# Normed rows turned over by transposing DMAs in place of identity products and VectorE copies (tiles 4 to 15)

## The chip, the cores and the metric

The kernel runs on one core of a Trainium2 chip. The metric is the device time of one execution in microseconds (us); of several runs the median is taken. The engines are called as in the profile: PE is TensorE, PEld its weight loads, DVE is VectorE, ACT is ScalarE, POOL is GpSimd, SP is SyncE, which here only issues DMAs.

## The reference

The input x has 2048 rows of 512. It is normed once, and two branches read the normed rows xn; their sum is added to x.

```python
def _layernorm(x, axis=-1, eps=1e-5):
    m = jnp.mean(x, axis=axis, keepdims=True)
    v = jnp.var(x, axis=axis, keepdims=True)
    return (x - m) / jnp.sqrt(v + eps)

# _A_ref: H = 32 heads of Dh = 16
qkv = (x @ wqkv).reshape(B, S, 3, H, Dh).transpose(2, 0, 3, 1, 4)
q, k, v = qkv[0], qkv[1], qkv[2]
p = softmax(einsum("bhqd,bhkd->bhqk", q, k) * Dh ** -0.5)
o = einsum("bhqk,bhkd->bhqd", p, v)
o.transpose(0, 2, 1, 3).reshape(B, S, D) @ wo

# _B_ref: a two-layer MLP over the rows' axis
h = _layernorm(x)
u = gelu(einsum("bsd,sf->bdf", h, w1) + b1)
(einsum("bdf,fs->bds", u, w2) + b2).transpose(0, 2, 1)

xn = _layernorm(x)
x + _A_ref(xn, wqkv, wo) + _B_ref(xn, w1, b1, w2, b2)
```

All tensors are bf16. The products with wqkv need xn with its 512 features on the partitions, that is, xn turned over; the MLP needs it as it is.

## The kernel before

The 2048 rows are 16 tiles of 128. Each tile t has a slice `xn_sb[:, t, :]` (128 rows by 512 features) and a slice of `xnT4` (128 features by 4 blocks of features by 128 rows), its turned-over copy. For tiles 0 to 3 a prologue turns every tile over by itself. For tiles 4 to 15 this is done in pairs, while attention is already running on the tiles that are there.

For such a pair (a, a + 1) the steps are: statistics (`ln_stats`, DVE) and the reciprocal deviation (`ln_rstd`, ACT, two small instructions, lines 611 and 614); the norm (`ln_norm`, DVE, line 630); `tr_steps`, which turns both tiles over; `kt_steps`, the K products of the pair (PE, four groups of four matmuls) and their copy (DVE); and `v_steps`, the V products of each tile (PE) with a copy and a scaling (DVE). `tr_steps` has three steps: `transpose_pe` for the one tile and for the other (PE, four products with the identity `ident` each, line 687, into one bank of PSUM), and `transpose_copy` (DVE, line 700), which copies the two turned tiles from PSUM to `xnT4`. `kt_mm` and `v_mm` (both through `mm_full`, line 667) and `qt_mm` read `xnT4`.

Attention goes by blocks of 512 queries and four heads: `score_mm` (PE, line 770) writes scores into banks of PSUM, `exp_tile` (ACT, line 783) takes one to three banks at a time, `pv_mm` (PE, line 795) multiplies by V. Some exponentials are instead made on DVE and POOL (`first_planes` and `make_plane`, lines 847 and 857).

The order of all this from the first K products on is written out by hand in the string `ORDER`, which `replay` reads: a letter C with a chain's number takes the next step of that chain (the chains are the lists of steps above, in the order of `chains`), S issues scores, E an exponential, P four products with V. The order of the string is thus the program order of every engine: PE, DVE, ACT, POOL and SP each run their own instructions strictly in that order. `Sched.add` records every operation with the keys that it reads and writes; `Sched.plan` turns each dependence on another engine, or on a DMA, into a semaphore wait of the later instruction. A DMA is an operation of the engine that issues it: SP waits for what the DMA needs, and all that SP has to issue later stands behind it. `q_steps` has such DMAs: it spreads the Q rows of two blocks of heads over `QT` (`QT<-qraw`), and the first of them stands between tiles 13 and 14 in the program.

When a chain's first step is taken, the string also names its PSUM bank. For the six `tr` chains this bank is written by the identity products and freed by the copy.

Later in the program `ln2_norm` scales `xn_sb` in place for the MLP (line 644), and the memory of `x_sb`, `xn_sb` and three quarters of `xnT` is used again for planes of the exponentials.

Of the kernel before, what the change touches and what calls it, by code (L numbers as in the profile page):

```python
# [430 lines left out]
def bass_parallel_sum__softmax_full_mha__mixer_token_mlp__prompt_kernel(  # L431
# [18 lines left out]
    with ExitStack() as es:  # L450
        block = es.enter_context(nc.Block())

        def sb(name, shape, dt):
            return es.enter_context(nc.sbuf_tensor(name, shape, dt))
# [3 lines left out]
        x_sb = x_flat[:, :].rearrange("p (t d) -> p t d", d=D)  # L458
        xn_sb = xn_flat[:, :].rearrange("p (t d) -> p t d", d=D)
# [3 lines left out]
        xnT4 = xnT_flat[:, :].rearrange("p (b ct n) -> p b ct n", b=NQB, ct=NCT)  # L463
# [29 lines left out]
        mv = sb("mv", [128, NT, 4], F32)  # L493
# [7 lines left out]
        sc = Sched(nc, es)  # L501
# [20 lines left out]
        for j in range(32):  # L522
# [6 lines left out]
               writes=[("jcol",)])  # L529
        for q in range(4):  # L530
            sl = slice(32 * q, 32 * q + 32)
            sc.add("dve", lambda e, sl=sl: e.tensor_tensor(ident[sl, sl], jrow[sl, 0, :], jrow[sl, 1, :], ALU.is_equal),
                   reads=[("jcol",), ("ident0",)] + [("jrow", j) for j in range(32)], writes=[("ident", q)])
# [93 lines left out]
                          reads=[("x", t), ("nmean", t)], writes=[("mv", t), ("qraw", 1)])  # L627

        def ln_norm(t):
            return sc.add("dve", lambda e: e.tensor_scalar(xn_sb[:, t, :], x_sb[:, t, :], mv[:, t, 0:1], mv[:, t, 2:3],  # L630
                                                           ALU.add if t == T_ACT else ALU.subtract, ALU.mult),
                          reads=[("x", t), ("mv", t), ("rs", t)], writes=[("xn", t)])

        def ln2_scales():
            rk = [("rs", t) for t in range(NT)]
            sc.add("dve", lambda e: e.tensor_tensor(mv[:, :, 3], mv[:, :, 2], mv[:, :, 2], ALU.mult),
                   reads=rk, writes=[("s2",)])
            sc.add("act", lambda e: e.activation(mv[:, :, 3], mv[:, :, 3], ACTF.Ln, bias=epsb[:, 1:2], scale=-EPS),
                   reads=[("s2",), ("epsb", 1)], writes=[("s2",)])
            return sc.add("act", lambda e: e.activation(mv[:, :, 3], mv[:, :, 3], ACTF.Exp, scale=-0.5),  # L640
                          reads=[("s2",)], writes=[("s2",)])
# [42 lines left out]
        def transpose_pe(t, bk, off):  # L684
            op = None
            for ct in range(NCT):
                op = sc.add("pe", lambda e, ct=ct: e.transpose(
                    ps_bf[:, bk * 1024 + off + ct * 128: bk * 1024 + off + (ct + 1) * 128],
                    xn_sb[:, t, ct * 128:(ct + 1) * 128], ident[:]),
                    reads=[("xn", t)] + [("ident", q) for q in range(4)], writes=[("bank", bk)])  # L690
            return op
# [5 lines left out]
        def copy(eng, dst, src, reads, writes):  # L697
            if eng == "act":
                return sc.add("act", lambda e: e.activation(dst, src, ACTF.Identity), reads, writes)
            return sc.add("dve", lambda e: e.tensor_copy(dst, src), reads, writes)  # L700

        def transpose_copy(t0_, n_, bk, eng):
            c0 = 128 * (t0_ % 4)
            dst = xnT4[:, t0_ // 4, :, c0:c0 + 128 * n_].rearrange("p ct (t j) -> p t ct j", t=n_)
            src = ps_bf[:, bk * 1024: bk * 1024 + 512 * n_].rearrange("p (t ct j) -> p t ct j", t=n_, ct=NCT)
            return copy(eng, dst, src, [("bank", bk)], [("xnT", t) for t in range(t0_, t0_ + n_)])
# [184 lines left out]
        ln_var_act(T_ACT)  # L891
        ln_stats(1)
        ln_norm(0)
        transpose_pe(0, TBK[0], 0)
        zeros(N_ZERO1)
        ln_rstd(1, 2)
        ln_stats(3)
        ln_norm(1)
        transpose_pe(1, TBK[1], 0)
        const_v(0, 1)  # L900
        ln_rstd(2, 3)
        transpose_copy(0, 1, TBK[0], "dve")
        ln_norm(2)
        pro_q(0)
        transpose_pe(2, TBK[2], 0)
# [25 lines left out]
            return [lambda bk, t=t: ln_stats(t) for t in (a, a + 1) if t > 4] + [fin]  # L931

        def tr_steps(t0_):
            z = [lambda bk, i=i: transpose_pe(t0_ + i, bk, 512 * i) for i in range(2)]
            return z + [lambda bk: transpose_copy(t0_, 2, bk, "dve")]

        def kt_steps(T, t0_, n_):
            return [lambda bk, ct=ct: kt_mm(T, t0_, n_, ct, bk) for ct in range(NCT)] + [
# [105 lines left out]
        def yo_steps(st, idx):  # L1044
            qb, sti = divmod(st, 4)
            ob = idx % 2
            lastqb = qb == NQB - 1

            def yt(ft, bk):
                if ft == 0:  # L1050
                    dma("sp", xres[:, ob, :], x2[128 * st:128 * (st + 1), :], reads=[], writes=[("xres", ob)])
                yt_mm(bk, st, ft, ft == 0, lastqb and ft == NFT - 1)
                if ft == NFT - 1 and not lastqb:
                    w2_load()
            z = [lambda bk, ft=ft: yt(ft, bk) for ft in range(NFT)]
            if not lastqb:
                z += [lambda bk, T=T: op_mm(qb, sti, T, bk, False, T == 3) for T in range(4)]

                def fin(bk):
                    sc.add("dve", lambda e: e.tensor_tensor(osb[:, ob, :], bank(bk), xres[:, ob, :], ALU.add),  # L1060
                        [("bank", bk), ("xres", ob)], [("osb", ob)])
                    dma("sp", out2[128 * st:128 * (st + 1), :], osb[:, ob, :], reads=[("osb", ob)], writes=[("out", st)],
                        out_dma=True)
            else:
                def fin(bk):
                    sc.add("dve", lambda e: e.tensor_tensor(part[:, sti, :], bank(bk), xres[:, ob, :], ALU.add),
                        [("bank", bk), ("xres", ob)], [("part", sti), ("w1blk", 0), ("w1blk", 1)])
            return z + [fin]
# [69 lines left out]
        for a in range(4, NT, 2):  # L1138
            chains += [tr_steps(a), kt_steps(0, a, 2), v_steps(a, 2, 0, 1)]
# [18 lines left out]
        for i, st in enumerate(yt_order):  # L1158
            z = yo_steps(st, i)
# [228 lines left out]
```

## Time and profile before

| | us |
|---|---|
| median of 3 runs | 627.82 |
| lowest and highest of them | 627.67, 628.01 |
| the profiled execution, its whole time | 627.77 |
| its span (first to last instruction) | 626.0 |

| engine | busy us | share of the span | instructions |
|---|---|---|---|
| PE | 616.7 | 99% | 8777 |
| ACT | 614.2 | 98% | 698 |
| DVE | 584.1 | 93% | 909 |
| POOL | 431.5 | 69% | 624 |

Of the span, the first 9.5 us are the prologue up to the first scores. The tiles 4 to 15 are normed from 13.2 us (tile 4) to 34.2 us (tile 15) and turned over between 14.7 and 36.2 us. The granted TensorE clock is full throughout (0.999 on the mean).

In the rows shown below, a row of the time line has the start and the length in us, the engine, the line of the kernel, the operation, the tile it writes and the tiles it reads, their shapes, and how many instructions in a row were merged into it; in brackets stands the idle time of the engine before it and what ended that. Consecutive rows of one engine can overlap a little, since the next instruction is started before the last has ended. "SPq" is the time for which SP was issuing a DMA, not the time of the transfer. A row of the DMA issues has the number of issues, the size of one and, last, the median time from issue to landing.

### The profile page before, as it was taken

The numbers are of one execution on the slowest core, as the hardware profiler recorded it, in microseconds if no ns is written. First come the engines' busy times: TensorE is split into PE (matmuls) and PEld (weight loads), VectorE is DVE, ScalarE is ACT, GpSimd is POOL, SyncE is SP. The second block draws the span as 40 slices with busy tenths as digits, with TensorE's granted clock in tenths as the row PEclk, the third lists the DMA queues.
The fourth block names the chain that finished last, engine by engine and source line by source line (L and its number), as shares of the span: only waits on it lengthen the run. The fifth ranks groups of instructions, "written<-read, shape, count | busy, mean of one in ns | idle before, by whom it ended". The sixth has DMA issues, their size and how long they took to land.

```text
span 626.0 us, 20540 instructions
## 1 busy us (share of the span) xinstructions
PE 616.7 (99%) x8777; PEld 195.3 (31%) x8777; DVE 584.1 (93%) x909; ACT 614.2 (98%) x698; POOL 431.5 (69%) x624
## 2 busy tenths in 40 slices
PE   8999999999999999999999999999999999999997
PEld 3544333232222222222323332222222222322222
DVE  7999999989999999999999988998989999999996
ACT  8999999999999999999999999999999999999996
POOL 2105766766767767769789777777857788888784
PEclk9999999999999999999999999999999999999999
DMA  8001210112202121030120031213131021222001
GB/s 237 4 12 40 50 54 6 39 39 55 54 11 63 37 66 40 21 78 12 28 52 24 18 87 38 60 39 76 42 91 42 19 59 46 50 52 67 20 27 45
DMA packets 69514, 29.74 MB, mean 48 GB/s; under 512 B 56182, under 2 KB 66422, under 8 KB 69422
## 3 DMA queue, kind: packets, MB, share of 16 engines
q1 hardware_dynamic: 68990, 28.03, 18.3%
q8 instruction: 69, 1.13, 0.8%
q10 hardware_dynamic: 432, 0.39, 0.2%
q14 instruction: 23, 0.19, 0.1%
HBM read 21.88 MB, written 2.59 MB: 39 GB/s over the span
## 4 chain that ended last, share of the span: by engine, by line
PE 82%; ACT 11%; DVE 6%; issue 0%; POOL 0%; DVEq 0%; POOLq 0%
PE ps L795 33%; PE ps L770 28%; PE ps L667 20%; ACT pT L783 8%; ACT wqkv_sb L783 3%; DVE planes L847 1%; DVE x_sb L847 1%; DVE xn_sb L847 1%; DVE stats L604 1%; DVE xn_sb L630 0%; DVE xnT L700 0%; DVE xnT L847 0%; DVE zer L1086 0%; ACT mv L611 0%; ACT mv L614 0%
## 5 line engine op out<-in xcount | busy, mean ns | idle before, releaser
L783 ACT ACTIVATE pT<-ps 128x1024 bf16<-128x1024 f32 (+2 forms) x488 | 459.7, 1034 | 2.2 <-PE ps L770 1.5
L770 PE MATMUL ps<-QT,KT 32*128 32x512 bf16 x2048 | 253.3, 384 | 1.5 <-ACT pT L783 0.4
L847 DVE TENSOR_SCALAR planes<-ps 128x512 int16<-128x512 f32 (+1 forms) x268 | 200.2, 776 | 14.7 <-PE ps L660 6.9
L783 ACT ACTIVATE wqkv_sb<-ps 128x1024 bf16<-128x1024 f32 (+2 forms) x172 | 174.8, 1039 | 0.1
L795 PE MATMUL ps<-pT,V 128*32 128x512 bf16 x950 | 157.7, 386 | 0.6 <-DVE V L700 0.6
L847 DVE TENSOR_SCALAR x_sb<-ps 128x512 int16<-128x512 f32 (+1 forms) x190 | 139.7, 765 | 8.0 <-PE ps L770 3.2
L770 PEld LDWEIGHTS ps<-QT,KT 32*128 32x128 bf16 x2048 | 65.9, 91 | 238.2 <-ACT pT L783 145.8
L795 PE MATMUL ps<-planes,V 128*32 128x512 bf16 x574 | 116.1, 384 | 0.0
L795 PE MATMUL ps<-x_sb,V 128*32 128x512 bf16 x477 | 98.1, 383 | 0.0
L857 POOL INT64_ADD planes<-planes x79 | 60.5, 771 | 43.3 <-DVE planes L847 36.4
L795 PE MATMUL ps<-wqkv_sb,V 128*32 128x512 bf16 x335 | 83.3, 386 | 0.0
L795 PE MATMUL ps<-planes,V17b 128*32 128x512 bf16 x314 | 77.4, 384 | 0.1
L857 POOL INT64_ADD planes<-x_sb x80 | 59.2, 745 | 23.6 <-DVE x_sb L847 22.0
L847 DVE TENSOR_SCALAR xnT<-ps 128x512 int16<-128x512 f32 (+1 forms) x89 | 69.4, 808 | 1.3 <-PE ps L660 0.6
L857 POOL INT64_ADD x_sb<-planes x64 | 53.0, 832 | 20.3 <-DVE planes L847 17.6
L847 DVE TENSOR_SCALAR xn_sb<-ps 128x512 int16<-128x512 f32 (+1 forms) x73 | 58.3, 816 | 4.5 <-PE ps L770 2.9
L795 PE MATMUL ps<-x_sb,V17b 128*32 128x512 bf16 x219 | 56.8, 384 | 0.0
L667 PE MATMUL ps<-gT,w2blk 128*32 128x512 bf16 (+1 forms) x688 | 53.0, 383 | 0.0
L795 PEld LDWEIGHTS ps<-pT,V 128*32 128x32 bf16 x950 | 39.3, 94 | 38.2 <-issue 35.1
L667 PE MATMUL ps<-xn_sb,w1blk 128*32 128x512 bf16 x624 | 50.4, 383 | 0.0
L795 PE MATMUL ps<-xnT,V 128*32 128x512 bf16 x204 | 49.0, 383 | 0.0
L795 PE MATMUL ps<-xn_sb,V 128*32 128x512 bf16 x203 | 43.8, 383 | 0.0
(125 smaller groups left out, 898.5 us busy)
## 6 DMA issues: line engine op xcount, KB each, us to landing
w1blk<-in_B_w_dram SPq DMA_DIRECT2D x10, 512.0 KB
w2blk<-in_B_w_dram SPq DMA_DIRECT2D x16, 320.0 KB
denb<-rec_scr SPq DMA_DIRECT2D x15, 256.0 KB
xres<-in_A_x_dram SPq DMA_DIRECT2D x16, 128.0 KB, 3.1
QT<-qraw SPq DMA_DIRECT2D x120, 16.0 KB, 1.8
OT<-OT SPq DMA_DIRECT2D x60, 32.0 KB, 2.5
out_dram<-osb SPq DMA_DIRECT2D x12, 128.0 KB, 2.3
x_sb<-in_A_x_dram SPq DMA_DIRECT2D x2, 512.0 KB
```

The costliest lines, as they stand in the source:

```text
L604: sc.add("dve", lambda e: e.bn_stats(stats[:, t, :], x_sb[:, t, :]), reads=[("x", t)], writes=[("stats", t)])
L667: op = sc.add("pe", lambda e, sl=sl, c=c: e.matmul(dst[sl, :], lhsT=lhsT[:, sl], rhs=rhs, start=start, stop=stop, tile_position=(0, 32 * c ...
L770: return sc.add("pe", lambda e: e.matmul(bank(bk), lhsT=KT[32 * r:32 * r + 32, T, 128 * kt:128 * (kt + 1)], rhs=QT[32 * r:32 * r + 32, slo ...
L783: return sc.add("act", lambda e: e.activation(slots(us), pick(ps3, bs), ACTF.Exp, scale=EXP_SCALE), reads=[("bank", b) for b in bs], write ...
L795: return sc.add("pe", lambda e: e.matmul(bank(PV_BANK)[32 * r:32 * r + 32, :], lhsT=vt_[:, off:off + 32], rhs=rhs, start=start, stop=stop, ...
L847: return sc.add("dve", lambda e: e.tensor_scalar(pick(plane_i[pb].rearrange("p (r n) -> p r n", n=512), ss), pick(ps3, bs), BIAS + SHIFT[0 ...
L857: return sc.add("pool", lambda e: e.int64_add(plane_q[pb][:, 0:128 * n], plane_q[pb0][:, 0:128 * n], -down * LANES), reads=rd, writes=wr, ...
```

## The change

`ln_norm` now also issues, for tiles from 4 on, one DMA on SP's queue that reads the normed tile in SBUF and writes it turned over into `xnT4`, with the keys (`xn`, `xnT`) that the copy had. The three steps of `tr_steps` do nothing; they are kept, so that the string `ORDER` still finds them. The products of the pair now wait for two DMAs in place of one copy. The prologue's tiles 0 to 3 are as before.

```diff
         def ln_norm(t):
-            return sc.add("dve", lambda e: e.tensor_scalar(xn_sb[:, t, :], x_sb[:, t, :], mv[:, t, 0:1], mv[:, t, 2:3],
+            op = sc.add("dve", lambda e: e.tensor_scalar(xn_sb[:, t, :], x_sb[:, t, :], mv[:, t, 0:1], mv[:, t, 2:3],
                                                            ALU.add if t == T_ACT else ALU.subtract, ALU.mult),
                           reads=[("x", t), ("mv", t), ("rs", t)], writes=[("xn", t)])
+            if t >= 4:
+
+                sc.add("sp", lambda e: e.dma_start(xnT4[:, t // 4, :, 128 * (t % 4):128 * (t % 4) + 128], xn_sb[:, t, :],
+                                                   transpose=True),
+                       reads=[("xn", t)], writes=[("xnT", t)], dma=True)
+            return op
...
         def tr_steps(t0_):
-            z = [lambda bk, i=i: transpose_pe(t0_ + i, bk, 512 * i) for i in range(2)]
-            return z + [lambda bk: transpose_copy(t0_, 2, bk, "dve")]
+            return [lambda bk: None] * 3
```

The lines behind line 630 move down by six, so that line 667 becomes 673, 770 becomes 776 and 795 becomes 801.

SP's queue, from the last loads of the prologue to the QT copies of the first `q_steps`, before:

```order
L516 DMA wqkv_sb<-in_A_wqkv_dram 128x4x128 x2
L516 DMA wqkv_sb<-in_A_wqkv_dram 128x4x384
L516 DMA wqkv_sb<-in_A_wqkv_dram 128x4x256 x2
L516 DMA QT<-qraw 16x512 [waits s_pool,s_dve]
L516 DMA QT<-qraw 16x512 x3
L516 DMA QT<-qraw 16x512 [waits s_pool]
```

The same place of SP's queue in the changed program, in which `s_dve` is DVE's semaphore:

```order
L516 DMA wqkv_sb<-in_A_wqkv_dram 128x4x128 x2
L516 DMA wqkv_sb<-in_A_wqkv_dram 128x4x384
L516 DMA wqkv_sb<-in_A_wqkv_dram 128x4x256 x2
L635 DMA_TRANSPOSE xnT<-xn_sb 128x4x128 [waits s_dve] x10
L516 DMA QT<-qraw 16x512 [waits s_pool,s_dve]
L516 DMA QT<-qraw 16x512 x3
L635 DMA_TRANSPOSE xnT<-xn_sb 128x4x128 [waits s_dve] x2
```

Ten transposes, each of which waits for its norm, now stand ahead of the first QT copies, and two behind the first four.

PE before, from the identity products of tiles 6 to 9 to the first K products of tiles 6, 7 (the last two rows):

```order
L687 MATMUL ps<-ident,xn_sb 128x128 [waits s_act,s_dve]
L687 MATMUL ps<-ident,xn_sb 128x128 x3
L770 MATMUL ps<-QT,KT 128x512
L660 MATMUL ps<-xnT,wqkv_sb 128x512 [waits s_pe]
L687 MATMUL ps<-ident,xn_sb 128x128 [waits s_dve]
L687 MATMUL ps<-ident,xn_sb 128x128 x3
L770 MATMUL ps<-QT,KT 128x512 [waits s_act]
L770 MATMUL ps<-QT,KT 128x512 x2
L660 MATMUL ps<-xnT,wqkv_sb 128x512 [waits s_pe]
L795 MATMUL ps<-pT,V 32x512 x4
L667 MATMUL ps<-xnT,wqkv_sb 32x256 [waits s_dve]
L667 MATMUL ps<-xnT,wqkv_sb 32x256 x15
```

PE in the changed program at the same place; `dqi0` to `dqi3` are the semaphores of the four DMAs:

```order
L776 MATMUL ps<-QT,KT 128x512 [waits s_act]
L666 MATMUL ps<-xnT,wqkv_sb 128x512 [waits s_pe]
L776 MATMUL ps<-QT,KT 128x512 [waits s_act]
L776 MATMUL ps<-QT,KT 128x512 x2
L666 MATMUL ps<-xnT,wqkv_sb 128x512 [waits s_pe]
L801 MATMUL ps<-pT,V 32x512 [waits s_dve]
L801 MATMUL ps<-pT,V 32x512 x3
L673 MATMUL ps<-xnT,wqkv_sb 32x256 [waits dqi0,dqi1]
L673 MATMUL ps<-xnT,wqkv_sb 32x256 x15
L673 MATMUL ps<-xnT,wqkv_sb 32x256 [waits dqi2,dqi3,s_act]
L673 MATMUL ps<-xnT,wqkv_sb 32x256 x7
```

The identity products between the scores are gone, and the K products of the two pairs wait for two DMAs each where they waited for a DVE copy.

## The prediction

> **What bounds the kernel now.** I read first the busy time of every engine in chosen stretches (us busy, then the number of instructions), and then the list of waits.
>
> ```profile
> 20.00:30.00 10.00, 9.50 (x194) 5.07 (x190) 9.65 (x27) 9.88 (x18) 2.34 (x7) 1.00 0.02 5
> 30.00:40.00 10.00, 8.57 (x216) 4.68 (x217) 9.33 (x30) 9.18 (x17) 0.00 (x0) 1.00 0.06 15
> 40.00:600.00 560.00, 559.32 (x7765) 169.72 (x7753) 529.74 (x775) 559.11 (x614) 410.58 (x549) 1.00 0.19 44
> ```
> ```profile
> ACT pT L783 <- PE ps L770: 1.5, 3, 0.8
> ```
>
> The columns are PE, PEld, DVE, ACT, POOL, then the granted clock and the DMA share. From 40 to 600 us ACT is busy for 559.11 of 560 us, with exponentials alone, and in the whole run its exponentials wait only 1.5 us for scores. A modelled PE also shows 559.32, but a busy PE need not be PE at its peak, while ACT's instructions follow one another without a gap. So **ACT is the pacemaker**: what the change does not take from or give to ACT's idle time before 40 us does not reach the end, and what it does take is not won back. Between 20 and 40 us ACT idles 0.12 + 0.82 us. That is nearly all there is to gain.
>
> **What is removed.** The rows of the removed work, by line and by tile (nanoseconds least, median, most):
>
> ```profile
> L687 PE MATMUL ps<-ident,xn_sb x48: 216/219/231, 14.7 to 35.1; 128*128 128x128 bf16 x48
> L630 DVE TENSOR_SCALAR xn_sb<-x_sb,mv x12: 402/406/415, 13.2 to 33.8; 128x512 bf16<-128x512 bf16 x12
> ```
> ```profile
> L700 DVE COPY xnT<-ps x6: 658/670/684, 16.2 to 35.5; 128x1024 bf16<-128x1024 bf16 x6
> ```
> ```profile
> 20.07 0.84 PE L687 MATMUL ps<-ident,xn_sb 128*128 128x128 bf16 x12
> ```
>
> DVE loses 6 copies of 0.67 us, 4.0 us in all. PE loses 48 products; twelve of them pass in 0.84 us, so 48 take 48/12 x 0.84 = 3.4 us. Both lie beside ACT's exponentials, so neither sum is a saving by itself. The twelve norms (0.41 us each) stay where they are on DVE. Added are twelve DMAs of 128 KB on SP's queue, each behind its norm.
>
> [...]
>
> **What a transposing transfer costs.** The trace has none. The nearest rows are the issues on SP and the times from issue to landing:
>
> ```profile
> 1.64 1.53 SPq L516 DMA_DIRECT2D wqkv_sb<-in_A_wqkv_dram  x3
> 3.21 2.08 SPq L516 DMA_DIRECT2D x_sb<-in_A_x_dram  x4
> 5.34 5.98 SPq L516 DMA_DIRECT2D wqkv_sb<-in_A_wqkv_dram  x5
> ```
> ```profile
> 30.89 0.60 SPq L516 DMA_DIRECT2D QT<-qraw  x1
> ```
> ```profile
> QT<-qraw SPq DMA_DIRECT2D x120, 16.0 KB, 1.8
> OT<-OT SPq DMA_DIRECT2D x60, 32.0 KB, 2.5
> ...
> wqkv_sb<-in_A_wqkv_dram SPq DMA_DIRECT2D x5, 128.0 KB, 3.2
> ```
>
> Call s the time that one issue holds SP, and r the time from the end of the issue to the landing. For s the ends are 0.5 (1.53/3, a load of the same 128x4x128 shape) and 1.2 (5.98/5, the same behind a full queue). For r they are 1.2 (1.8 - 0.60, SBUF to SBUF) and 2.7 (3.2 - 0.5). I take **s = 1.0 and r = 1.5**: the transfer runs from SBUF to SBUF, which is r's lower end plus something for eight times the bytes, and it turns rows into columns on top of being as finely cut as the loads, which puts s near its upper end. I add 0.1 us for the two hand-overs (norm to SP, landing to PE), an estimate. Transfers from one queue are issued one after the other, so the n-th of a group lands at (end of the first norm) + 0.1 + n s + r.
>
> **Five meeting places.** The K products of a pair of tiles are PE's first readers, and PE works in order: while it waits, the scores behind wait too, and ACT runs dry once the scores in PSUM are used up. For each place I set the landing against the latest start that leaves ACT fed.
>
> Tiles 4, 5 (DVE, PE, ACT):
>
> ```profile
> 13.16 0.41 DVE L630 TENSOR_SCALAR xn_sb<-x_sb,mv 128x512 bf16<-128x512 bf16 x1 [1.50 <-ACT mv L614]
> ...
> 16.95 0.62 PE L667 MATMUL ps<-xnT,wqkv_sb 128*32 128x256 bf16 x16
> ...
> 18.16 0.39 PE L770 MATMUL ps<-QT,KT 32*128 32x512 bf16 x2
> ...
> 19.24 4.34 ACT L783 ACTIVATE pT<-ps 128x1024 bf16<-128x1024 f32 x5
> ```
>
> The scores behind are ready at 18.55 and taken at 19.24, so 16.95 may slip to about 17.57. Landing: 13.57 + 0.1 + 2.0 + 1.5 = 17.17. Cost 0.
>
> Tiles 6 to 9, four transfers in a row:
>
> ```profile
> 18.94 0.74 DVE L630 TENSOR_SCALAR xn_sb<-x_sb,mv 128x512 bf16<-128x512 bf16 x2
> ...
> 22.84 0.12 PEld L667 LDWEIGHTS ps<-xnT,wqkv_sb 128*32 128x32 bf16 x8 [0.26 <-DVE xnT L700]
> ...
> 23.17 0.39 PE L770 MATMUL ps<-QT,KT 32*128 32x512 bf16 x3
> ...
> 24.07 3.87 ACT L783 ACTIVATE pT<-ps 128x1024 bf16<-128x1024 f32 x6
> ```
>
> Tiles 8 and 9 are first read at 22.84; the scores behind are ready at 23.56 for an exponential at 24.07. Of that half microsecond I count 0.25, an estimate, since everything up to the next scores slips too: the limit is 23.1. Landing of the fourth: 19.35 + 0.1 + 4.0 + 1.5 = 24.95. **Cost 1.85.**
>
> Tiles 10, 11:
>
> ```profile
> 24.74 0.41 DVE L630 TENSOR_SCALAR xn_sb<-x_sb,mv 128x512 bf16<-128x512 bf16 x1
> ...
> 28.18 0.83 PE L667 MATMUL ps<-xnT,wqkv_sb 128*32 128x256 bf16 x20
> ...
> 28.95 0.39 PE L770 MATMUL ps<-QT,KT 32*128 32x512 bf16 x1
> ```
> ```profile
> 29.18 1.08 ACT L783 ACTIVATE pT<-ps 128x512 bf16<-128x512 f32 x2
> ```
>
> The score is ready at 29.34 and the second of these exponentials, which takes it, begins near 29.66: limit 28.43. Landing: 25.15 + 3.6 = 28.75. Cost 0.32.
>
> Tiles 12, 13, the one place with a gain:
>
> ```profile
> 28.40 0.73 DVE L630 TENSOR_SCALAR xn_sb<-x_sb,mv 128x512 bf16<-128x512 bf16 x2
> ...
> 32.39 0.68 DVE L700 COPY xnT<-ps 128x1024 bf16<-128x1024 bf16 x1
> 32.99 0.42 DVE L700 CAST V<-ps 128x256 bf16<-128x256 f32 x1
> ...
> 33.12 0.62 PE L667 MATMUL ps<-xnT,wqkv_sb 128*32 128x256 bf16 x16 [1.08 <-DVE xnT L700]
> 33.32 0.41 DVE L630 TENSOR_SCALAR xn_sb<-x_sb,mv 128x512 bf16<-128x512 bf16 x1
> ...
> 34.99 8.12 ACT L783 ACTIVATE pT<-ps 128x512 bf16<-128x512 f32 x12 [0.50 <-PE ps L770]
> ```
>
> Here the copy came late, PE stood for 1.08 us and ACT then for 0.50. Landing now: 28.81 + 3.6 = 32.41, 0.7 before 33.12, so the 0.50 goes. **Gain 0.50.** Limit for it: 32.6.
>
> Tiles 14, 15: the norm at 33.32 moves up by the missing copy (32.99 - 32.39 = 0.60) and ends at 33.13.
>
> ```profile
> 36.24 0.29 PE L667 MATMUL ps<-xnT,wqkv_sb 128*32 128x256 bf16 x4 [0.29 <-DVE xnT L700]
> 36.46 0.39 PE L770 MATMUL ps<-QT,KT 32*128 32x512 bf16 x3
> ```
> ```profile
> 36.45 1.53 ACT L783 ACTIVATE pT<-ps 128x1024 bf16<-128x1024 f32 x2
> ```
>
> The second exponential takes these scores near 37.35 (they are ready at 36.85); with ACT 0.5 earlier the slack is gone and the limit is 36.2. Landing: 33.13 + 3.6 = 36.73. Cost 0.53.
>
> The QT copies now stand behind ten transfers on SP and are issued a little later; their first reader is the third block of scores, after the 128 products of the two blocks before it, so I cost this at nothing. It would cost only if SP fell behind by tens of microseconds.
>
> **Sum:** 0 + 1.85 + 0.32 - 0.50 + 0.53 = +2.2 us, on the profiled execution's own 627.77 us (its span of 626.0 and 1.8 around it, 0.05 under the median of 627.82): **630.0 us**.
>
> **Rivals.**
> 1. *Ordinary transfers* (the other side: not slower). With s = 0.5 and r = 1.2 the fourth of tiles 6 to 9 lands at 19.35 + 0.1 + 2.0 + 1.2 = 22.65, before 23.1; every other place is met too, and the 0.50 is kept: 627.3. It decides at s = 0.59 or below with that r (23.1 - 19.45 - 1.2 = 2.45 for four). For it: the load of the same shape issues in 0.51 us. Against: no row turns rows into columns. [...]
> 2. *One at a time*: a transfer begins only when the one before has landed, 2.5 us each (the OT row). Costs 1.10, 6.35, 1.82, 1.31, 2.03, less 0.50 = 12.1: 639.9. For it: the 1.8 to 3.2 us of the landing rows. Against: the loads at the start overlap, five issues in 5.98 us.
> 3. *PE is the pacemaker after all*: then 3.4 us of products and the waits of 1.08 and 0.29 go from its stream: 623.0. Against: ACT's 559.11 of 560.
> 4. That the change does not do what it says is shut out by the order of the instructions, in which the transfers stand and the products do not.
>
> **How the numbers follow.** Forecast 0.50, rival 1 0.30, rival 2 0.17, rival 3 0.03. The forecast's bounds: s = 1.2 and r = 2.7 cost 1.20 + 3.85 + 1.92 + 1.41 + 2.13 - 0.50 = 10.0, so 637.8; below, it runs into rival 1. The range 627.0 to 637.8 leaves out rivals 2 and 3. A measurement of this kernel tells about 0.2%, 1.26 us, from no change. Rival 3 and the tip of rival 1 are faster: 0.04. Rival 1 and the cheap end of the forecast (0.05) are within: 0.34. The rest is slower: 0.62.
>
> **What would show it.** In the changed profile: SP's issues of the transposes near 1.0 us each and landings about 1.5 us behind; PE waiting for a DMA at the products of tiles 8 and 9 for about 2 us, and less at 10, 11 and 14, 15; the 1.08 us wait of tiles 12, 13 gone; ACT idle by about 2.2 us more between 20 and 40 us, and as full as before after 40. Issues of 0.5 us and no such wait would be rival 1, landings each 2 us or more behind the one before rival 2. The forecast is wrong if ACT shows idle time after 40 us that it did not have.

## Result, and the profile after

| | before | after |
|---|---|---|
| median of 3 runs, us | 627.82 | 635.54 |
| lowest and highest, us | 627.67, 628.01 | 635.35, 635.58 |
| the profiled execution, us | 627.77 | 635.35 |
| its span, us | 626.0 | 633.4 |

The ratio is 1.0122 (95% interval 1.0099 to 1.0145): the change makes the kernel slower by 7.7 us. (The profiled execution's span is 7.4 us longer, 0.1 of it ahead of the first exponential; the other 7.3 are taken apart below.) The forecast was 630.0 with a range of 627.0 to 637.8. The sign and the mechanism held; the size, +2.2 us, was too small by a factor of three and a half.

The busy time of the engines after, from the page's first part; DVE is busy for 3.2 us less than before, ACT for 0.7 us more:

```profile
PE 617.0 (97%) x8729; PEld 193.5 (31%) x8729; DVE 580.9 (92%) x903; ACT 614.9 (97%) x698; POOL 430.6 (68%) x624
```

The stretches of the changed kernel (columns as in the prediction: PE, PEld, DVE, ACT, POOL, then the granted clock and the DMA share):

```profile
20.00:30.00 10.00, 7.68 (x181) 3.48 (x169) 5.74 (x18) 6.63 (x10) 2.33 (x7) 0.89 0.27 55
30.00:40.00 10.00, 7.11 (x150) 3.17 (x146) 7.96 (x25) 8.90 (x19) 0.00 (x0) 1.00 0.37 65
40.00:50.00 10.00, 7.94 (x177) 3.82 (x175) 6.67 (x23) 7.50 (x12) 0.00 (x0) 0.83 0.15 32
50.00:60.00 10.00, 10.00 (x276) 5.03 (x276) 9.09 (x17) 10.00 (x13) 2.45 (x3) 1.00 0.01 4
```

ACT was busy for 9.88 and 9.18 us of the first two before; now for 6.63, 8.90 and 7.50 us in three, and full from 50 us on. The list of waits between 9 and 55 us says for what (time, number of waits, longest):

```profile
DVE KT L706 <- PE ps L673: 10.0, 6, 2.7
PE ps L673 <- DMA xnT<-xn_sb: 6.9, 5, 2.1
ACT pT L789 <- PE ps L776: 6.6, 6, 2.4
```

PE waits for the transposing transfers, ACT for the scores that stand behind on PE. The five waits are the five meeting places of the prediction. PE's time line, the first K products of each:

```profile
18.97 1.05 PE L673 MATMUL ps<-xnT,wqkv_sb 128*32 128x256 bf16 x16 [1.84 <-DMA xnT<-xn_sb]
...
27.27 0.40 PE L673 MATMUL ps<-xnT,wqkv_sb 128*32 128x256 bf16 x8 [1.33 <-DMA xnT<-xn_sb]
...
33.46 0.84 PE L673 MATMUL ps<-xnT,wqkv_sb 128*32 128x256 bf16 x20 [0.94 <-DMA xnT<-xn_sb]
...
37.70 0.62 PE L673 MATMUL ps<-xnT,wqkv_sb 128*32 128x256 bf16 x16 [0.76 <-DMA xnT<-xn_sb]
...
42.41 0.29 PE L673 MATMUL ps<-xnT,wqkv_sb 128*32 128x256 bf16 x4 [2.06 <-DMA xnT<-xn_sb]
```

The transfers themselves, first the rows of line 635 (nanoseconds of one issue, least, median and most; then from the start of the issue to the landing), then SP's time line:

```profile
L635 SPq DMA_TRANSPOSE xnT<-xn_sb x12: 1189/1264/1361, 13.7 to 39.8; - x12
...
DMA to landing us min/median/max: 2.5/2.8/4.6
```
```profile
13.72 21.90 SPq L635 DMA_TRANSPOSE xnT<-xn_sb  x10
35.97 2.51 SPq L516 DMA_DIRECT2D QT<-qraw  x4
38.53 2.57 SPq L635 DMA_TRANSPOSE xnT<-xn_sb  x2
```

One issue holds SP for 1.26 us, just beyond the upper end of 1.2 that the prediction gave it. Six of the twelve transfers land 2.5 us after their issue began (1.25 after it ended), three near 3.2 and three 3.8 to 4.6 us.

ACT's time line shows the stalls that follow, among them two at the last place, and DVE's the norms of tile 6 (with 7) and of tile 14:

```profile
21.88 1.02 ACT L789 ACTIVATE pT<-ps 128x1024 bf16<-128x1024 f32 x1 [2.42 <-PE ps L776]
...
28.04 1.51 ACT L789 ACTIVATE pT<-ps 128x1024 bf16<-128x1024 f32 x2 [1.03 <-PE ps L776]
...
43.27 1.51 ACT L789 ACTIVATE pT<-ps 128x512 bf16<-128x512 f32 x2 [1.30 <-PE ps L776]
...
45.85 4.56 ACT L789 ACTIVATE pT<-ps 128x512 bf16<-128x512 f32 x6 [1.07 <-PE ps L776]
```
```profile
20.41 0.73 DVE L630 TENSOR_SCALAR xn_sb<-x_sb,mv 128x512 bf16<-128x512 bf16 x2
...
37.80 0.40 DVE L630 TENSOR_SCALAR xn_sb<-x_sb,mv 128x512 bf16<-128x512 bf16 x1
```

**Where the 7.3 us come from.** Each exponential can be found in both traces, and its start after less its start before is ACT's lateness. It changes only at the five places. What each adds, in us, for the changed kernel and for the experiments below (net of the start of the first exponential):

| kernel | tiles 4, 5 | 6 to 9 | 10, 11 | 12, 13 | 14, 15 | sum |
|---|---|---|---|---|---|---|
| forecast | 0 | 1.85 | 0.32 | -0.50 | 0.53 | 2.2 |
| changed kernel | 2.88 | 1.28 | 0.81 | -0.60 | 2.93 | 7.3 |
| e4b, nothing turned | 0 | -0.16 | 0 | -0.60 | 0 | -0.76 |
| e3, transfers that nobody reads | 0 | 0 | 0 | 0 | 0 | 0 |
| e1, tiles 4, 5 by products | 0 | 4.57 | 0.70 | -0.60 | 3.68 | 8.3 |
| e5, one transfer a pair | 1.06 | 0.34 | 0.32 | -0.27 | 0 | 1.45 |
| e9, the same from tile 6 on | 0 | 0.86 | 0.88 | -0.27 | 0 | 1.46 |
| e7, two transfers a tile | 5.41 | 7.64 | 2.84 | 0.71 | 6.64 | 23.2 |
| e2, waits filled | 1.57 | 3.42 | 0.79 | -0.61 | 3.11 | 8.3 |
| e8, waits filled better | 2.38 | 2.23 | 0.76 | -0.60 | 2.56 | 7.3 |
| e11, loads behind | 3.32 | 1.31 | 0.79 | -0.60 | 4.90 | 9.7 |
| e12, fetches moved | 0 | 3.95 | 1.01 | -0.60 | 5.14 | 10.6 (1.1 of it ahead of tile 4) |
| e10, only tiles 12, 13 | 0 | 0 | 0 | -0.43 | 0 | -0.43 |

From 50 us to the end the lateness of the changed kernel stays between 7.28 and 7.36 us: nothing is won back, and nothing more is lost.

### The profile page after: what moved, and what is told of

It reads as the page before. It is cut to its first block, busy times and chain, and to the rows that moved or that the text cites. A ratio compares the mean times of both kernels' runs of the same rounds, so it can differ in the third digit from the quotient of the medians.

```text
span 633.4 us, 20450 instructions
## 1 busy us (share of the span) xinstructions
PE 617.0 (97%) x8729; PEld 193.5 (31%) x8729; DVE 580.9 (92%) x903; ACT 614.9 (97%) x698; POOL 430.6 (68%) x624
## 4 chain that ended last, share of the span: by engine, by line
PE 82%; ACT 9%; DVE 6%; DMA 2%; issue 0%; SPq 0%
PE ps L801 33%; PE ps L776 28%; PE ps L673 21%; ACT pT L789 6%; ACT wqkv_sb L789 3%; DMA xnT<-xn_sb 2%; DVE x_sb L853 1%; DVE planes L853 1%; DVE stats L604 1%; DVE xn_sb L853 1%; DVE xn_sb L630 1%; DMA x_sb<-in_A_x_dram 0%; DVE xnT L853 0%; DVE KT L706 0%; DVE V L706 0%; DVE mv L606 0%
## 5 line engine op out<-in xcount | busy, mean ns | idle before, releaser
L673 PE MATMUL ps<-xnT,wqkv_sb 128*32 128x512 bf16 (+3 forms) x600 | 40.0, 350 | 7.5 <-DMA xnT<-xn_sb 6.9
```

The lines of the kernel that those rows point to most:

```text
L673: op = sc.add("pe", lambda e, sl=sl, c=c: e.matmul(dst[sl, :], lhsT=lhsT[:, sl], rhs=rhs, start=start, stop=stop, tile_position=(0, 32 * c ...
```

## Experiments

Each time stands beside runs of the kernel before on the same chip (medians 627.80 to 627.89).

### What could be won at all: e4b and e4

e4b leaves the turning of tiles 4 to 15 out, and Q, K and V of those tiles are made from the turned rows of tiles 0 to 3:

```diff
-            if t >= 4:
-                sc.add("sp", lambda e: e.dma_start(xnT4[:, t // 4, ...], xn_sb[:, t, :], transpose=True), ...)
...
-                            xnT4[:, t0_ // 4, ct, 128 * (t0_ % 4):128 * (t0_ % 4 + n_)], 128, 128 * n_, ...
+                            xnT4[:, 3, ct, 128 * (t0_ % 4):128 * (t0_ % 4 + n_)], 128, 128 * n_, ...
```

> Again without any turning over of tiles 4 to 15, and without zeros: the Q, K and V of these tiles are computed from the turned rows of tiles 0 to 3 instead, so nothing is written by POOL. The earlier kernel of this kind lost 6.4 us at its start, where a norm on DVE took 4.89 us beside POOL's memset, and then won 0.77 back by 40 us. Theory (ACT is the pacemaker, the memset was the artefact): 627.1 us, 626.8 to 627.5. Rival (the work taken from PE and DVE is what costs, by a lower clock): 630 us or more; second rival (PE is the pacemaker): 623 to 624.

Measured: 627.03 us, ratio 0.9987 (0.9978 to 0.9996). Its stretches:

```profile
20.00:30.00 10.00, 7.61 (x166) 3.52 (x162) 8.15 (x24) 9.94 (x18) 2.34 (x7) 1.00 0.02 5
30.00:40.00 10.00, 8.80 (x243) 4.81 (x241) 9.14 (x31) 9.68 (x18) 0.00 (x0) 1.00 0.06 15
```

PE is rid of 1.9 us between 20 and 30 us, and ACT gains 0.06. **ACT is the pacemaker**, shown; rival 3 of the prediction (623.0) falls. All that any way of turning these tiles could gain is 0.8 us, 0.60 of it at tiles 12, 13.

e4 was a first attempt at the same: tiles 4 to 15 read zeros, which POOL writes during the prologue.

```diff
+        for j in range(1, NQB):
+            memset("pool", xnT_flat[:, 2048 * j:2048 * (j + 1)], 0.0, [("xnT", 4 * j + q) for q in range(4)])
```

> The changed kernel without its transposing DMAs: tiles 4 to 15 are not turned over at all, their turned copies are zeros written by POOL at the start, so that neither PE and DVE do the work nor anybody waits for it. Theory (ACT is the pacemaker): only the 0.5 us come back that ACT waited near 35 us: 627.3 us, 626.8 to 627.6. Rival (PE's stream is the pacemaker, so its 3.4 us of products and the waits of 1.08 and 0.29 count): 623 to 624 us.

Measured: 632.71 us, ratio 1.0074 (1.0059 to 1.0089); neither. DVE's and POOL's time lines:

```profile
5.01 4.89 DVE L630 TENSOR_SCALAR xn_sb<-x_sb,mv 128x512 bf16<-128x512 bf16 x1
...
10.63 0.38 DVE L630 TENSOR_SCALAR xn_sb<-x_sb,mv 128x512 bf16<-128x512 bf16 x1
```
```profile
4.47 5.29 POOL L520 MEMSET xnT<- 128x2048 bf16 x3
```

A norm of 0.4 us lasted 4.89 us while POOL filled SBUF beside it, and the prologue ended 6.4 us later. So its time says nothing of the change; behind its prologue it gains the same 0.77 us as e4b.

### Whether the transfers cost by themselves: e3

The kernel before, with the twelve transfers added; they write to memory that nobody reads at that time.

```diff
+            if t >= 4:
+                spare = w1_flat[:, 512 * (t % 4):512 * (t % 4) + 512].rearrange("p (ct j) -> p ct j", j=128)
+                sc.add("sp", lambda e: e.dma_start(spare, xn_sb[:, t, :], transpose=True),
+                       reads=[("xn", t)], writes=[("spare", t % 4), ("w1blk", 0)] if t == 15 else [("spare", t % 4)], dma=True)
```

> The kernel before, which turns all tiles over on PE and DVE, with the twelve transposing DMAs added, into memory that nobody reads and that a later load overwrites. Theory (a transfer costs only whom it keeps waiting): 627.8 us, within 0.4. Rival (the transfers themselves slow others, by SP's queue, by the DMA engines or by SBUF): some us of the 7.7 show here too, 630 us or more.

Measured: 627.86 us, ratio 0.9999 (0.9989 to 1.0008). The same issues stand in the trace:

```profile
L635 SPq DMA_TRANSPOSE w1blk<-xn_sb x12: 1190/1258/2365, 13.8 to 37.1; - x12
...
DMA to landing us min/median/max: 2.4/2.6/4.9
```

They delay no exponential by more than 0.01 us. So a transfer costs here only what its reader waits. The QT copies stand behind the transfers here too, so what the prediction put at nothing for them is shown.

### Whether SP's time goes by instruction or by size: e7

Each tile turned by two transfers of two squares (128x128) each.

```diff
+            for h in range(2 if t >= 4 else 0):
+                sc.add("sp", lambda e, h=h: e.dma_start(
+                    xnT4[:, t // 4, 2 * h:2 * h + 2, 128 * (t % 4):128 * (t % 4) + 128],
+                    xn_sb[:, t, 256 * h:256 * h + 256], transpose=True), ...)
```

> The changed kernel with two transposing DMAs for each tile, two blocks of 128 features each: 24 issues of half the size. Theory (SP's 1.27 us are for the squares of an issue, so half of them take about 0.65): the same time, 634.5 to 636.5 us. Rival (they are for the instruction, whatever its size): a pair takes 5.1 us to issue in place of 2.5, tiles 6 to 9 10.2 in place of 5.1: 2.5 us more at each of four places and 5 at the fifth, 645 us or more.

Measured: 651.22 us, ratio 1.0369 (1.0355 to 1.0384); the rival.

```profile
L634 SPq DMA_TRANSPOSE xnT<-xn_sb x24: 1168/1246/2348, 13.6 to 55.4; - x24
...
  PE ps L673: 20.3, 6
...
DMA to landing us min/median/max: 2.3/2.4/4.4
```

Half the size takes 1246 instead of 1264 ns to issue. **The 1.25 us are for the instruction**, and landing is 0.2 to 0.4 us earlier: 2.3 us after the issue began at the least and 2.4 in the median, instead of 2.5 and 2.8.

### Whether the five places add up: e1, e5 and e9

e1 turns tiles 4 and 5 by products and a copy again:

```diff
-            if t >= 4:
+            if t >= 6:
...
+            if t0_ >= 6:
+                return [lambda bk: None] * 3
+            z = [lambda bk, i=i: transpose_pe(t0_ + i, bk, 512 * i) for i in range(2)]
+            return z + [lambda bk: transpose_copy(t0_, 2, bk, "dve")]
```

> The changed kernel, with tiles 4 and 5 turned over by PE and DVE again; tiles 6 to 15 by transposing DMAs. Theory (each meeting place adds its own stall, and nothing is won back or moved on): the 2.5 us by which the exponential behind the products of tiles 4 and 5 was late in the changed kernel go, the rest stays: 633.0 us, 632.7 to 633.4. The landing there was the slowest of all (2.6 us after the issue), beside the last loads. Rival (the stall is moved to the next place, since SP and the chip are as busy as before): 635 us or more.

Measured: 636.72 us, ratio 1.0143 (1.0127 to 1.0160), against 635.54 with all six pairs: the rival. PE's time line from the first wait on:

```profile
23.79 1.05 PE L673 MATMUL ps<-xnT,wqkv_sb 128*32 128x256 bf16 x16 [1.32 <-DMA xnT<-xn_sb]
...
26.15 0.62 PE L673 MATMUL ps<-xnT,wqkv_sb 128*32 128x256 bf16 x8 [1.31 <-DMA xnT<-xn_sb]
...
27.65 1.92 PE L673 MATMUL ps<-wqkv_sb,xnT 128*32 128x128 bf16 x64
```

The 2.88 us at tiles 4, 5 are gone, and tiles 6 to 9 cost 4.57 instead of 1.28 (table). In the changed kernel the stall at tiles 4, 5 makes ACT and its scores late by 2.88 us, but the norms of tiles 6 and 7 only by 1.47 (20.41 against 18.94 us). So part of the time that the next four transfers need had been waited for already, and the places don't add. In the changed kernel ACT's lateness behind tiles 6 to 9 is nearly the landing there less the limit that the trace of before gives: 27.2 - 23.1 = 4.1 us, and the table has 2.88 + 1.28 = 4.16. In e1 the fourth transfer lands earlier, at 26.1 us, which by itself would make 3.0 us; the other 1.6 of its 4.57 go with the granted clock, which was at half from 23.25 to 30.08 us in e1 and full there in the changed kernel (the table under e2 and e8 has all places):

```profile
23.25:30.08 6.83, 4.98 (x106) 2.83 (x106) 2.16 (x7) 2.34 (x5) 0.05 (x1) 0.50 0.20 41
```

e5 turns the first tile of every pair by a transfer and the second by products, so that no transfer stands behind another of its pair; e9 does so from tile 6 on:

```diff
-            if t >= 4:
+            if t >= 4 and t % 2 == 0:
...
+            return [lambda bk: None, lambda bk: transpose_pe(t0_ + 1, bk, 0),
+                    lambda bk: transpose_copy(t0_ + 1, 1, bk, "dve")]
```

> Of each pair the first tile (4, 6, 8, 10, 12, 14) is turned over by a transposing DMA, the second by PE and DVE as before: six DMAs, never two behind each other without a norm and more between them. Theory (what counts is whether the landing, norm + 0.1 + n x 1.27 + 1.25 us, meets PE's latest start): tile 8, the tightest, lands at 20.72 + 1.27 + 1.25 = 23.2 against 23.1, all the others meet theirs, so of the 7.7 us nothing is left, and some of the 0.5 us at tiles 12, 13 is won: 627.3 to 628.0 us. Rival (every transposing DMA costs its share, 7.7/12 each): 631.7 us.

Measured: 629.18 us, ratio 1.0022 (1.0013 to 1.0030); neither, though far nearer to the theory. Of 7.7 us 1.4 remain. Tile 4 is waited for:

```profile
18.41 0.62 PE L673 MATMUL ps<-xnT,wqkv_sb 128*32 128x256 bf16 x16 [1.45 <-DMA xnT<-xn_sb]
```

> The kernel with one transposing transfer per pair, now only for tiles 6, 8, 10, 12 and 14; tiles 4 and 5 are turned by products and a copy as before. Theory (what was left with one transfer per pair, +1.4 us over before, is for the most part the late landing of tile 4 beside the last loads): the 0.9 us at tiles 4, 5 goes and no other place has a transfer behind another, so 627.6 to 628.3 us. Rival (what is saved at tiles 4, 5 is lost again at tiles 6 to 9, as it was with both tiles of a pair): 629.0 us or more.

Measured: 629.02 us, ratio 1.0018 (1.0010 to 1.0027); the rival again, at its lower edge. The 1.06 us at tiles 4, 5 are gone, and tiles 6 to 11 cost 1.74 instead of 0.66. In both kernels what is left behind tiles 10, 11 goes by one landing, that of tile 10 (29.90 us in e5, 30.04 in e9). **A queue of transfers behind one another is most of the loss** (6 of 7.3 us), since six issues in place of twelve take it away, and with it the fall of the clock, which stays at 1.00 in e5 and e9; a place by itself is not a term that can be struck out of the sum.

### Whether the clock makes it worse: e2 and e8

In the changed kernel the granted clock falls at the first and the last of the five stalls (1.84 and 2.06 us); at the three between, of 0.76 to 1.33 us, it stays at 1.00:

```profile
19.00:22.00 3.00, 3.00 (x58) 1.75 (x62) 1.94 (x7) 0.55 (x4) 0.00 (x0) 0.50 0.00 0
...
42.00:46.60 4.60, 4.19 (x74) 2.10 (x78) 2.30 (x8) 2.26 (x4) 0.00 (x0) 0.63 0.08 18
...
42.63:46.04 3.41, 3.41 (x62) 1.70 (x62) 1.81 (x7) 1.70 (x3) 0.00 (x0) 0.50 0.08 20
```

The 0.63 is the mean of a stretch that is longer than the fall: the clock was at 0.50 from 18.74 to 22.15 and from 42.63 to 46.04 us, 3.4 us each time. At clock 0.50 the sixteen K products of tiles 4, 5 took 1.05 us instead of 0.62. e2 and e8 keep PE busy with products of ones while it waits (in e2 8, 5, 4, 3 and 9 of them ahead of the K products of tiles 4, 8, 10, 12 and 14; in e8 8, 5, 4, 3, 2 and 9 ahead of those of tiles 4, 6, 8, 10, 12 and 14):

```diff
+            fill = {4: 8, 8: 5, 10: 4, 12: 3, 14: 9}.get(t0_, 0) if T == 0 and n_ == 2 else 0
+            def mm(ct, bk):
+                if ct == 0:
+                    for _ in range(fill):
+                        warm_mm(bk)
+                kt_mm(T, t0_, n_, ct, bk)
```

> The changed kernel, with 29 matmuls of a matrix of ones in all (8, 5, 4, 3 and 9) put on PE ahead of the K products of tiles 4, 8, 10, 12 and 14, into the bank that those products then overwrite, so that PE works where it waited for a DMA. Theory (part of the loss is the TensorE clock, which was granted at 0.50 in the 3 us behind the first stall and at 0.63 in the 4.6 us behind the last): 0.8 us come back at tiles 4, 5 and 1.1 at tiles 14, 15: 633.6 us, 633.2 to 634.2, and a full clock there. Rival (the waits are all of it): 635.5 us or a little more.

Measured: 635.50 us, ratio 1.0125 (1.0103 to 1.0146); the rival. At tiles 4, 5 the clock stayed at 1.00 and the cost fell from 2.88 to 1.57 us: so 1.3 us of that place were the clock. All of it and more is lost at tiles 6 to 9 (3.42), where the clock was now at 0.50 from 24.48 to 27.89 us.

> The changed kernel with matmuls of ones in PE's waits again, now also ahead of the products of tile 6 (8, 5, 4, 3, 2 and 9 at tiles 4, 6, 8, 10, 12 and 14). In the first trial the products of tiles 4, 5 ran at the full clock (0.62 in place of 1.05 us), but PE then stood unfilled at tile 6, the clock fell to 0.52, and the five matmuls at tile 8 took 2.19 us in place of 1.1. Theory (the clock is part of the loss at tiles 14, 15, and what is won earlier is lost to the landings of tiles 6 to 9, which do not move): full clock throughout, 634.0 us, 633.3 to 634.8. Rival (the waits are all of it): 635.5 us or more.

Measured: 635.68 us, ratio 1.0127 (1.0112 to 1.0143), at a mean clock of 0.999; the rival. The stretch from 20 to 30 us, and the first and the last place:

```profile
20.00:30.00 10.00, 8.87 (x195) 4.07 (x187) 5.37 (x16) 6.37 (x9) 2.34 (x7) 1.00 0.27 55
```
```profile
19.83 0.62 PE L673 MATMUL ps<-xnT,wqkv_sb 128*32 128x256 bf16 x16 [0.92 <-DMA xnT<-xn_sb]
...
43.87 0.29 PE L673 MATMUL ps<-xnT,wqkv_sb 128*32 128x256 bf16 x4 [1.11 <-DMA xnT<-xn_sb]
```

With the clock full everywhere the sum is the same 7.3 us. That does not show that the slow clock costs nothing, for the landings of e8 were later than those of the changed kernel: 19.78 instead of 18.93 us for tile 5, 43.83 instead of 42.31 for tile 15. The table has, for three places, the landing of the last tile less the prediction's limit (17.57, 23.1 and 36.2 us), then ACT's lateness behind the place (here with the start of the first exponential, 0.1 us and in e12 0.8), then the clock behind it (half is 0.50, full 1.00):

| kernel | tiles 4, 5 | 6 to 9 | 14, 15 |
|---|---|---|---|
| changed kernel | 1.4, 3.0, half | 4.1, 4.3, full | 6.1, 7.4, half |
| e1 | no transfer | 3.0, 4.7, half | 7.1, 8.5, half |
| e2 | 1.4, 1.7, full | 3.7, 5.1, half | 8.6, 8.4, full |
| e8 | 2.2, 2.4, full | 4.5, 4.7, full | 7.6, 7.4, full |
| e11 | 1.8, 3.4, half | 4.5, 4.7, full | 7.2, 9.8, half for 6.8 us |
| e12 | 1.6, 1.9, full | 4.5, 5.9, half | 9.0, 11.4, half for 6.8 us |

**Where the clock is full, ACT is late by the landing less the limit, within 0.3 us; where it is at half, by 1.3 to 2.6 us more.** At the last place, behind which nothing changes any more, the half clock costs the changed kernel about 1.5 us of its 7.3 (7.4 - 6.1, against -0.2 at a full clock). e8 saved that and lost it again to a landing that came 1.5 us later.

### Why tile 5 landed late: e11 and e12

Tiles 4 and 5 landed 4.6 and 3.8 us after their issues began, six of the others 2.5. (The trace has sixteen landings for each transfer, as many as there are DMA engines, here called its shares; PE started behind the last of them, for tile 5 at 18.97 us behind 18.93.) The first guess was the last loads of wqkv, which still run then. e11 issues these three behind the transfers:

```diff
-        ld_w("sp", 2, 1, 4)
-        ld_w("sp", 1, 2, 4)
-        ld_w("sp", 0, 2, 4)
...
+            if t == 5:
+                ld_w("sp", 2, 1, 4)
+                ld_w("sp", 1, 2, 4)
+                ld_w("sp", 0, 2, 4)
```

> The changed kernel with the last three loads of wqkv issued behind the transfers of tiles 4 and 5 instead of ahead of them. Theory (tile 5 landed 2.6 us behind its issue because of these loads): tile 5 lands near 17.7 us instead of 18.9, the K products of tiles 4, 5 wait under 0.8 us instead of 1.84, and ACT's start behind them moves by under 1 us instead of 2.5. By the second part of the theory (what is saved at one place is lost at the next, since the norms of tiles 6 to 9 are not held up by PE's stall) the whole stays at 635 to 636.5 us. Rival 1 (another cause than the loads): the landing stays near 18.9 us and the time at 635.5. Rival 2 (the places add up after all): 633.5 us or less.

Measured: 637.52 us, ratio 1.0149 (1.0134 to 1.0165). The loads were out of the way (DMA share 0.02 and 0.00 from 13 to 15 us), tile 5 landed later still, at 19.37 instead of 18.93 us, and PE waited longer; so the theory fell:

```profile
13.00:14.00 1.00, 0.78 (x11) 0.12 (x8) 0.75 (x2) 0.99 (x2) 0.00 (x0) 1.00 0.02 4
14.00:15.00 1.00, 0.59 (x7) 0.23 (x7) 1.00 (x4) 1.00 (x2) 0.00 (x0) 1.00 0.00 1
```
```profile
19.41 1.05 PE L674 MATMUL ps<-xnT,wqkv_sb 128*32 128x256 bf16 x16 [2.31 <-DMA xnT<-xn_sb]
```

In both kernels an instruction fetch falls on this place, a packet of the queue that the profile lists as "q8 instruction". The DMA view of the changed kernel from 16.2 to 18.4 us: the mean busy share of the 16 DMA engines in 40 slices, and the queues (packets, MB, share):

```profile
DMA  9013799999998999990109001010010101000000
...
q1 hardware_dynamic: 551, 0.13, 71.5%
q8 instruction: 1, 0.02, 2.9%
q14 instruction: 1, 0.01, 2.8%
```

The transfer of tile 5 fills the engines from 16.4 to 17.2 us; behind that, from 17.26 to 18.01 us, 27 pieces of 256 bytes come one at a time, by the count the rest of one engine's share (512 pieces for 16 engines are 32 each). The packet of queue q8 (16 KB, 1.0 us) began at 16.2 us. In e11's trace it began at 15.7 and took 1.4 us: of the sixteen shares of tile 4 fifteen had landed by 16.3 us, the last at 18.1, and none of tile 5's ahead of that. Queue q8's packets come once in some 257 instructions of PE and PEld in the changed kernel (68 packets of 16 KB in the whole run for the 17,458 instructions on the page; between two packets the trace has 158 to 328 of them, 254 in the median). e12 therefore moves them by 128 instructions, about half of that:

```diff
-        for i in range(N_ZERO0):
+        for i in range(9):
             warm_mm(7)
+        for i in range(67):
+            r = i % 4
+            sc.add("pe", lambda e, r=r: e.matmul(bank(7)[32 * r:32 * r + 32, 0:128], lhsT=ones_w[:, 0:32], ...), ...)
```

> The changed kernel with PE's instruction fetches moved: of the twelve warming products at the start nine stay, and 67 narrow ones take the place of three, 64 more in all, or 128 instructions with their weight loads, half of the 256 that one fetch of 16 KB brings. Theory (one of the 16 DMA engines is held for 1.0 to 1.4 us by the fetch on queue q8 at 16.3 us, just when the transfers of tiles 4 and 5 move, and its share lands that much later): the fetch falls 2 us or more earlier or later, the transfers of tiles 4 and 5 land 2.5 to 3.2 us after their issue instead of 4.2 and 3.8, PE's wait of 1.84 us at tiles 4, 5 falls under 1.1 us and ACT's start behind them moves by under 1.8 us instead of 2.5; the whole, since what is saved there is lost at tiles 6 to 9, 634.5 to 636. Rival (the late landing has nothing to do with the fetch): landings of about 4 us, the wait of 1.84 and the 2.5 us stay.

Measured: 638.17 us, ratio 1.0159 (1.0142 to 1.0176). PE's time line:

```profile
13.92 1.46 PE L673 MATMUL ps<-wqkv_sb,xnT 128*32 128x128 bf16 x45 [1.10 <-issue]
...
19.20 0.62 PE L673 MATMUL ps<-xnT,wqkv_sb 128*32 128x256 bf16 x16 [0.24 <-DMA xnT<-xn_sb]
```

The fetch fell near 15 us, ahead of tile 5's issue (16.66 to 17.90 us in the trace). Tile 5 landed 2.5 us after its issue began, all sixteen shares within 0.2 us, instead of 3.8, and tile 4 3.4 instead of 4.6 (its issue alone took 2.22). PE's wait fell from 1.84 to 0.24 us and the place cost nothing, as the theory had it. One thing blurs this last number: PE itself had stood for 1.10 us at 13 us with nothing to wait for that the profile shows, the first scores came 0.7 us later, and the clock was at 0.50 from 13.58 to 17.00 us, so PE and ACT came to the place later; the landings counted from their issues are free of that. The total was missed by 2 us: tiles 6 to 9 cost 3.95 instead of 1.28, as in e1 and e2, and tiles 14, 15 5.1 instead of 2.93; at the last place, here and in e11 (4.90), the clock was at half for 6.8 us instead of 3.4:

```profile
44.30:51.13 6.83, 5.80 (x81) 2.41 (x81) 2.69 (x9) 3.02 (x4) 0.00 (x0) 0.50 0.11 24
```

The same holds at tile 13 in the changed kernel: a packet of q8 at 35.2 us took 0.9 us, tile 12's last share landed 1.6 us behind its others, and tile 13 behind that, 2.0 us after the end of its issue. In the trace of e8 it is tile 14: a packet of q8 at 41.2 us, the last share 1.5 us behind the others, and tile 15 behind that. The packets of the other instruction queue, q14 (8 KB), go with smaller delays: at tiles 7 and 10 of the changed kernel, with packets at 24.0 and 31.4 us, and at tile 10 in the traces of e5 and e9, with packets at 28.5 and 28.0, one share landed 0.65 to 1.3 us behind its others. No run was made to move those.

### The one gain alone: e10

Only tiles 12 and 13 are turned by transfers:

```diff
-            if t >= 4:
+            if t in (12, 13):
```

> Only tiles 12 and 13 are turned by transfers, the one place at which the changed kernel gained; all others as before. Theory: PE's wait of 1.08 us for the late copy goes and ACT's wait of 0.50 us at 35 us with it, the two issues of 1.27 us end early enough (landing 28.8 + 0.1 + 2.5 + 1.3 = 32.7 us against 33.1), and DVE is 0.7 us earlier at tile 14's norm: 627.2 to 627.5 us, a ratio near 0.999. Rival (the gain came only because the stalls ahead of it had moved the scores): 627.8 us, as before, or a little above it.

ACT's time line of e10 (before, six exponentials were split here by a wait of 0.50 us at 34.99), and the stretch:

```profile
32.97 4.06 ACT L789 ACTIVATE pT<-ps 128x512 bf16<-128x512 f32 x6
```
```profile
30.00:40.00 10.00, 8.67 (x247) 5.07 (x249) 9.31 (x31) 9.60 (x18) 0.00 (x0) 1.00 0.19 41
```

The wait is gone, and ACT is 0.43 us earlier from there to the end. The median is 627.41 us against 627.87, but the ratio, 1.0004 (0.9994 to 1.0013), can't tell the two apart: seven runs lie between 627.29 and 628.05 us at a granted clock of 1.000, and four between 628.51 and 630.27 at 0.994 to 0.997, which none of the 21 runs of before shows. What lowers the clock in these was not found. So the gain is in the trace and not established in the time.

## Why the prediction was right in sign and wrong in size

- **ACT as the pacemaker, the removed work worth nothing, nothing won back:** right. e4b shows the first two (1.9 us less of PE between 20 and 30 us give ACT 0.06), the constant lateness behind 50 us the third.
- **QT copies cost nothing:** right for themselves (e3). But SP needs 2.51 us for four of them, from 35.97 us, and the transfer of tile 14, whose norm ended at 38.20, was issued at 38.53: some 0.3 us of the cost at tiles 14, 15.
- **s = 1.0 us:** too small. It is 1.26, beyond the upper bound of 1.2, and goes by instruction (e7). The nearest row, the load of the same shape at 0.51, was far off, and that of the last five loads, at 1.20 beside busy DMA engines (share 1.04 to 1.22 from 6 to 12 us of the kernel before), near it by chance.
- **r = 1.5 us:** near for half of the transfers (1.25), and wrong where an instruction fetch ran beside the transfer: 2.6 at tile 5, 2.0 at tile 13 (e11, e12). The prediction took one r for all places; its upper end of 2.7 was the true one at the first place, which it costed at nothing.
- With these s and r the prediction's own sum is 1.24 + 2.68 + 0.61 + 0.35 + 0.82 = 5.7 us (tiles 4, 5: 13.57 + 0.1 + 2 x 1.27 + 2.6 - 17.57; tiles 12, 13 with r = 2.0: 33.45 - 32.6 - 0.50; the others alike with r = 1.25). **By that sum the mis-sized s and r are 3.5 of the missing 5.1 us.** That 635.5 lies in the range is in part luck: s lies outside its bounds, and the range reaches so high by r = 2.7 at every place, which the runs show at three transfers only (2.6 to 3.3 at tiles 4, 5 and 12).
- **Places that add up:** wrong. ACT's lateness behind a place is the landing there less its limit of before, and 1.3 to 2.6 us more where the clock is at half, not a cost added to what was lost ahead (e1, e5 against e9, the table under e2 and e8). This by itself makes the sum smaller, not larger.
- **A full clock:** the sum has no term for the clock. It was at 0.50 for 3.4 us behind the first and the last stall, which cost 1.3 us at the first place (e2) and about 1.5 at the last. That e8, at a full clock, is as late on the whole comes from its later landings.
- **Tiles 14, 15 (0.53 forecast, 2.93 measured):** the largest miss. The norm of tile 14 did not move up by 0.60: at 37.80 us it is 4.48 us later than before, as late as ACT. PE starts at 42.41, 4.2 behind that norm's end, not 3.6. With the QT copies that makes ACT 1.4 us later at the first stall there; the other 1.5 come as a second stall (ACT's 1.07 us at 45.85) while the clock is at 0.50. At that exponential ACT's lateness grows by 1.2 us in each of the changed kernel, e1, e7, e11 and e12, all with the clock at half, and by under 0.1 in e2 and e8, where it is full: this part is the clock. The 2.56 us of e8 are the landing of tile 15 alone.
- **Tiles 12, 13:** the gain of 0.50 came as 0.60, though PE still waited 0.76 us for the landing: ACT was already late by more than that.
- **The sign named for being wrong**, idle time of ACT after 40 us, did appear (7.50 of 10 us between 40 and 50). It is the fifth place, moved there by the stalls ahead, and no new one.
- **Rival 1, ordinary transfers (627.3):** fell on s, 1.26 us, far above the value at which it decides (2.45 us for four is 0.61 each, not the 0.59 that the prediction gives). In the trace a transposing transfer is slower than a plain load of the same shape at the issue, 1.26 us against 0.51, and for the bytes too: a tile's 512 pieces of 256 bytes pass the 16 engines in 0.75 us, 175 GB/s from 22.00 to 22.75 us, against 278 to 312 GB/s while the plain loads run from 12 to 14 us.
- **Rival 2, one at a time (639.9):** fell. In tiles 6 to 9 the issues follow one another at 1.28 us while each lands 2.5 to 3.2 us after its issue began.

## What to carry to other kernels

Where products and a copy on engines with slack are replaced by a DMA, price the issue of each DMA on its queue (1.26 us here), the landing (2.5 to 4.6 us after the issue began) and what else the DMA engines do at that moment; an instruction's removal from an engine with slack paid for none of it here (e4b: 0.06 us between 20 and 30 us for 1.9 us of PE). PE's products behind the four DMAs of tiles 6 to 9 had to wait for four issues here, from 20.8 to 26.0 us, so spread such DMAs over pairs or keep every second one on the old way (here 12 issues lose 7.7 us and 6 lose 1.4). When several stalls follow one another, compare each landing with the limit of the undisturbed run and take the lateness behind it from that, instead of adding costs; then look whether the granted clock fell there, which came on top (1.3 to 2.6 us here). A repair of the first stall alone can make the next one larger (e1: 4.57 us instead of 1.28).

## What the runs showed of the hardware that was not expected

- A transposing DMA from SBUF to SBUF holds SP for 1.26 us at the median (1.19 to 1.36 in the changed kernel, single issues up to 2.4 in e3 and e7), and the same for 128x256 as for 128x512 (1.25, e7); a plain load of 128x4x128 took 0.51.
- One instruction fetch of 16 KB took 0.9 to 1.5 us (the 68 packets of queue q8 in the changed kernel), and a transfer that moved beside it had fifteen shares on time and the last 1.5 to 1.9 us behind them (1.6 at tile 12 of the changed kernel; tile 4 of e11; tile 14 of e8); the shares of the next transposing transfer then landed only behind that last one. That the share waits for the fetch on its DMA engine is inferred from the times; with the fetch moved (e12) tile 5 landed 2.5 us after its issue began instead of 3.8.
- In the traces of the kernel before and after, the granted clock is 0.50 or 1.00 and nothing between. After the change it is at half for 3.4 us twice inside the run; 6.8 us at a time stand in e1, e11 and e12, 10.2 us in e7. In the changed kernel it fell at PE's stalls of 1.84 and 2.06 us and not at those of 0.76 to 1.33; in e1 two stalls of 1.3 us, 2.4 us apart, went with 6.8 us at half.
- A norm of 0.4 us on DVE lasted 4.89 us while POOL filled SBUF with zeros in three instructions of about 1.8 us (e4).
